# One column-block split of a product in two parts instead of three, and the order of the work around it

## The chip, the cores and the metric

One core of one Trainium2 chip. The metric is the device time of one execution in microseconds (us), median of the runs shown. Engines are named as in the profile: PE is TensorE's matrix products, PEld its weight loads, DVE VectorE, ACT ScalarE, POOL GpSimd, SP the queue that issues most DMAs.

## What is computed

Attention with a soft cap, and after it two feed-forward layers, on 896 tokens (2 sequences of 448) of width 768:

```python
scores = cap * tanh(scale * (q @ k.T) / cap);  attn = softmax(scores) @ v   # 12 heads of 64
x = attn laid out as [896, 768]
h = x @ w_in                                   # [896, 1024]
solu = h * softmax(h);  ln = layernorm(solu) * g_ln
x = ln @ w_out                                 # [896, 768]   <- the product that is changed
g = x @ w_gate;  out = (silu(g) * (x @ w_val)) @ w_out2
```

The weights come as 64-bit floats and are turned into 32-bit ones on the chip. Every large product is done as three: each operand is split into a high and a low part (`hi`, `lo`), and hi\*hi, hi\*lo and lo\*hi are added up.

## The kernel before

The program has stages that follow each other: the attention by pairs of heads, `ff1_h` (h, one of 7 token tiles of 128 at a time, on PE 36 products of 512 columns a tile), `ff1_T` (ln of a token tile is transposed into the tiles `lA`, `lB`, `lC`), `ff1_x2` (ln @ w_out), `ff2_gv` and `ff2_out`. PE leaves a result in one of 8 PSUM banks (pool `pm`); from there ACT writes the high part and DVE the low part of the transposed ln and of x.

**ln of a tile.** The tail of `ff1_h` (L354 to L391) takes the row maximum (DVE, L359), the exponentials with their sums (ACT, two halves of 512, L362), the product with h (DVE, L370), mean and variance (DVE; for tiles 5 and 6 ACT squares instead, L378), a power on POOL (L385) and the normalisation over 1024 columns (ACT for tiles 4 to 6, L388, else DVE). `ff1_T` (L395) then does 8 transposes on PE in two groups of 4, each group evicted to hi by ACT (L408) and to lo by DVE (L409). In the profile its PSUM tile is `lt`.

**w_out.** `load_w_out(j)` (L414) makes `wo_j`, the 128 output columns j of w_out, in two halves i of 512 rows each: a DMA, the conversion to 32 bits (ACT takes the absolute value, DVE clamps, shifts and joins in four instructions), four multiplications by g_ln on ACT (L422), the copy to hi on ACT (L423) and the rest to lo on DVE (L424). Rows 0 to 511 serve the contraction chunks fc 0 to 3, rows 512 to 1023 the chunks 4 to 7. Pool `wo` holds three such tiles, the raw and the 32-bit halves have two buffers each.

**The product.** `ff1_x2(j, get, N, o)` (L426) computes 128 output columns j for a block of N tokens that begins at o: 24 products (8 chunks fc times 3) of N columns, then hi by ACT (L435) and lo by DVE (L436). Before, the 896 tokens are three blocks: `lA` 384, `lB` 256, and `lC` 256, which lies in the tile `y`. That is 18 groups of 24 products.

**The order.** `steps` (L560 and L565) is the order in which the pieces are recorded. After `self.in_order = False` (L538) a scheduler moves instructions among each other, but a wait of one engine's queue holds all that stands behind it on that engine. Instructions of `load_w_out` up to the shift stay in program order (`pin=True`, L420). The stage around the change is 178.99 to 242.14 us of the trace: from the transposes of token tile 4 to the first product of `ff2_gv`.

Of the kernel before, what the change touches and what calls it, by code (L numbers as in the profile page):

```python
# [6 lines left out]
F32R = mybir.dt.float32r  # L7
# [29 lines left out]
class Kernel:  # L37
# [465 lines left out]
    def run(self):  # L503
        nc = self.nc
        KD, K1, K2, F1 = self.KD, self.K1, self.K2, self.F1
        self.raws, self.ln, self.wos, self.gvs, self.w2, self.a, self.wraw = {}, {}, {}, {}, {}, {}, {}

        st = self.st = self.pool("st", side="right")
        self.raw = self.pool("raw", side="right")
        self.at = self.pool("at", side="right")  # L510
        psc = self.psc = self.pool("psc", bufs=2, space=PSUM)
        ptA = self.pt = self.ph = self.pool("ptA", bufs=1, space=PSUM)
        self.attn_load(0, "kq")
        self.setup()
        self.w_in_load(0)
        self.attn_load(1, "kq")
        self.attn_load(0, "v")
        self.attn_load(1, "v")
        self.w_in_load(1)
        self.wi = [self.slot(f"wi{u}", [128, KD, F1], f"wi{u}") for u in range(2)]  # L520
        self.x = self.slot("x", [128, KD * 2 * 896], "x").rearrange("p (k u n) -> p k u n", k=KD, u=2)
        nc.sync.dma_start(self.gt, self.g_ln.rearrange("(f p) -> p f", p=128))


        w = [self.w_in_steps(i) for i in range(2 * KD)]
        none = lambda: None
        self.w_steps = [(w[i][1], w[i][2], w[i + 1][0] if i + 1 < 2 * KD else none, w[i][3]) for i in range(2 * KD)]
        self.attn_T(0)
        self.keep_warm(4)
        w[0][0]()  # L530
        h = [self.ff1_h(t) for t in range(7)]
        for i in range(2 * self.NP):
            self.attn_pair(i)
        self.htag = "t"
        self.attn_pair(2 * self.NP, [f for _, f in h[0][:3]])
        for _, f in h[0][3:]:
            f()
        self.in_order = False  # L538
        self.at.release()
        self.raw.release()  # L540
        ptA.release()
        psc.release()


        self.pt = self.ph = self.pool("pm", bufs=8, space=PSUM)
        self.htag, self.ttag = "m", "m"
        lA = self.slot("l", [128, K1, 2, 384], "lA")
        T = [self.ff1_T(t, lambda: lA, 128 * t) for t in range(3)]
        lp = self.pool("lp", side="right")
        self.wo = self.pool("wo", bufs=3, side="right")  # L550
        lB = lp.tile([128, K1, 2, 256], F32R, name="lB", tag="lB")
        self.y = self.slot("x", [128, KD * 2 * 896], "y")
        lC = self.y[:, :4096].rearrange("p (f u n) -> p f u n", f=K1, u=2)
        T3, T4 = self.ff1_T(3, lambda: lB, 0), self.ff1_T(4, lambda: lB, 128)
        T5, T6 = self.ff1_T(5, lambda: lC, 0), self.ff1_T(6, lambda: lC, 128)
        wo = [[(0.0, lambda j=j: self.load_w_out(j))] for j in range(KD)]
        blocks = ((lambda: lA, 384, 0), (lambda: lB, 256, 384), (lambda: lC, 256, 640))
        x2 = [[[self.ff1_x2(j, *blocks[n])] for n in range(3)] for j in range(KD)]

        steps = h[1] + T[0] + h[2] + T[1] + h[3][:2] + T[2] + h[3][2:] + h[4][:3] + wo[0] + h[4][3:] + wo[1] + h[5][:5] + T3 + h[5][5:] + h[6][:2] + T4 + h[6][2:]  # L560
        for _, f in steps:
            f()
        X = [self.slot(f"wi{u}", [128, 6144], f"x2_{u}") for u in range(2)]
        self.x2 = [X[j // 3][:, j % 3 * 1792:(j % 3 + 1) * 1792].rearrange("p (u n) -> p u n", u=2) for j in range(KD)]
        steps = x2[0][0] + x2[0][1] + wo[2] + x2[1][0] + T5 + x2[1][1] + T6 + x2[0][2] + x2[1][2]  # L565
        for j in range(2, KD):
            if j + 1 < KD:
                steps += wo[j + 1]
            if j >= KD - 2:
                steps += [(0.0, lambda i=j - KD + 2: self.load_gv(0, i))]  # L570
            steps += x2[j][0] + x2[j][1] + x2[j][2]
        for _, f in steps:
            f()
        self.wo.release()
        lp.release()


        ap = self.pool("ap", side="right")
        big = self.slot("l", [128, 6144], "a_0")
        ab = [big] + [ap.tile([128, 5376], F32R, name=f"a_{i}", tag=f"a_{i}") for i in range(1, 4)]  # L580
        w2x = self.y[:, :4608].rearrange("p (f u n) -> p f u n", f=6, u=2)
        for fc in range(K2):
            self.a[fc] = ab[fc // 3][:, fc % 3 * 1792:(fc % 3 + 1) * 1792].rearrange("p (u n) -> p u n", u=2)
        for fc in range(6):
            self.w2[0, fc] = w2x[:, fc]
        for i, t in enumerate([big] + X):
            self.w2[0, 6 + i] = t[:, 5376:].rearrange("p (u n) -> p u n", u=2)
        for fc in range(K2):
            for i, (N, o) in enumerate(((384, 0), (512, 384))):
                if fc + 1 < K2:  # L590
                    self.load_gv(fc + 1, i)
                elif i == 0:
                    for m in range(3):
                        self.w2[0, 9 + m] = self.y4(((fc - 1) % 2) * 2 + (m + 1) // 2).rearrange(
                            "p u k f -> p (u k f)").rearrange("p (m u n) -> p m u n", m=2, u=2)[:, (m + 1) % 2]
                    self.load_w2(0, 9, 1)
                    self.load_w2(0, 10, 2)
                if i == 1 and fc >= 2 and fc % 2 == 0:
                    self.load_w2(0, fc - 2, 2 if fc < 10 else 1)
                self.ff2_gv(fc, N, o)  # L600


        for fc in range(K2):
            self.w2[1, fc] = X[fc // 6][:, fc % 6 * 768:(fc % 6 + 1) * 768].rearrange("p (u n) -> p u n", u=2)
        nt = self.B * self.S // 128
        for half in range(2):
            for t in range(nt):
                if half == 0 and t < K2 // 2:
                    self.load_w2(1, 2 * t, 2)
                self.ff2_out(half, t)  # L610
        ap.release()
        st.release()
        self.pt.release()
        self.sb.release()
# [33 lines left out]
```

## Time and profile before

| | |
|---|---|
| time, median of 3 runs | 509.64 us (509.62 to 510.17) |
| the profiled execution | 509.62 us, its span 507.8 us |
| mean granted TensorE clock | 0.991 |
| PE busy | 98% of the span |
| DVE busy, ACT busy | 68%, 50% |
| DMA | 52.40 MB, mean 103 GB/s |

The span runs from the first to the last instruction of the trace; 1.8 us of the time lie around it. A busy share counts an engine as busy while any instruction of it is in work, and the end of a PE instruction is modelled, so how fast PE goes is read from the starts of its instructions. An instruction's time in the trace is longer than the distance to the next start where the two overlap; for queues that run full the distance of the starts is the cost.

### The profile page before, as it was taken

Reading aid. Unit: us, or ns where it says so; the run is one execution under the profiler, and the core shown is the slowest. Engines: PE = TensorE matmul, PEld = TensorE weight load, DVE = VectorE, ACT = ScalarE, POOL = GpSimd, SP = SyncE. Lnnn points to the kernel's source line nnn. Section 1 sums busy time; section 2 is a strip of 40 time slices with the busy share of each in tenths; the row PEclk is TensorE's granted clock in tenths of the full one; section 3 lists DMA queues with packets and bytes.
Section 4 is the critical chain, followed back from the end, with each engine's and each line's share of the span. In section 5 each row is a group of like instructions: output and inputs, shape, how many; then the busy total and the mean of one; then the engine's idle time right before and its main releaser. Section 6 shows DMA issues by size and latency. Waiting matters only on the chain.

```text
span 507.8 us, 7455 instructions
## 1 busy us (share of the span) xinstructions
PE 496.4 (98%) x2920; PEld 411.0 (81%) x2920; DVE 347.9 (68%) x625; ACT 256.4 (50%) x388; POOL 20.7 (4%) x63
## 2 busy tenths in 40 slices
PE   6999999999999999999999999999999999999996
PEld 5444544456788899999999988889999889999996
DVE  2788888873778895677899999897997868100000
ACT  2999999990313696474544444353444434100000
POOL 1111111110000000000000000000000000000000
PEclk7999999999999999999999999999999999999999
DMA  8945555310000222145354544435343525111111
GB/s 185 210 119 154 130 154 127 99 61 2 0 1 0 82 86 84 43 148 163 125 168 144 174 138 155 156 124 161 99 147 95 169 77 157 31 32 31 32 32 31
DMA packets 66916, 52.40 MB, mean 103 GB/s; under 512 B 35904, under 2 KB 62272, under 8 KB 66880
## 3 DMA queue, kind: packets, MB, share of 16 engines
q1 hardware_dynamic: 65184, 50.90, 35.6%
q10 hardware_dynamic: 1664, 1.02, 0.6%
q8 instruction: 23, 0.38, 0.3%
q14 instruction: 13, 0.11, 0.1%
q0 software_dynamic: 32, 0.00, 0.0%
HBM read 49.16 MB, written 2.75 MB: 102 GB/s over the span
## 4 chain that ended last, share of the span: by engine, by line
PE 93%; ACT 3%; DMA 2%; DVE 2%; issue 0%; ACTq 0%; POOL 0%; POOLq 0%
PE o L29 17%; PE g L29 17%; PE v L29 17%; PE x L29 10%; PE h L29 10%; PE pv L29 8%; PE sc L29 7%; PE S L29 4%; PE T L29 2%; DMA q<-in_q_dram 1%; PE lt L29 1%; ACT P L29 1%; DVE sm L29 1%; ACT wo L29 1%; DMA wo_raw<-in_moe_w_out_dram 1%; DVE e L29 0%
## 5 line engine op out<-in xcount | busy, mean ns | idle before, releaser
L29 PE MATMUL g<-x,y 128*128 128x512 f32 (+1 forms) x432 | 91.3, 363 | 0.0
L29 PE MATMUL v<-x,y 128*128 128x512 f32 (+1 forms) x432 | 90.5, 362 | 0.0
L29 PEld LDWEIGHTS g<-x,y 128*128 128x128 f32 x432 | 78.3, 188 | 8.8
L29 PEld LDWEIGHTS v<-x,y 128*128 128x128 f32 x432 | 78.2, 188 | 8.5
L29 PE MATMUL h<-wi,x 128*128 128x512 f32 x252 | 58.8, 392 | 0.0
L29 PEld LDWEIGHTS h<-wi,x 128*128 128x128 f32 x252 | 46.9, 188 | 10.9 <-issue 1.4
L29 PE MATMUL o<-x,a 128*128 128x384 f32 x294 | 52.4, 336 | 0.0
L29 PEld LDWEIGHTS o<-x,a 128*128 128x128 f32 x294 | 51.2, 188 | 0.0
L29 ACT ACTIVATE P<-sc,c 112x896 f32<-112x896 f32 x48 | 45.6, 1000 | 3.0 <-PE sc L29 2.8
L29 ACT ACTIVATE P<-P,cp 112x1792 f32<-112x1792 f32 x24 | 43.1, 1794 | 0.5
L29 PE MATMUL pv<-P,v 112*64 112x448 f32 x192 | 41.2, 551 | 0.0
L29 PEld LDWEIGHTS sc<-ks 64*112 64x112 f32 x288 | 24.0, 176 | 21.0 <-ACT P L29 9.0
L490 ACT ACTIVATE ob<-o 128x384 f32<-128x384 f32 x14 | 6.9, 494 | 65.1 <-PE o L29 65.1
L29 PE MATMUL sc<-ks 64*112 64x448 f32 x288 | 37.1, 388 | 2.0 <-ACT P L29 1.1
L29 PE MATMUL o<-y,a 128*128 128x384 f32 x189 | 34.3, 337 | 0.0
L29 PEld LDWEIGHTS o<-y,a 128*128 128x128 f32 x189 | 33.2, 188 | 0.1
L29 PEld LDWEIGHTS pv<-P,v 112*64 112x64 f32 x192 | 11.7, 136 | 23.9 <-issue 15.9
L29 PE MATMUL x<-lA,wo 128*128 128x384 f32 x144 | 28.1, 337 | 0.9 <-ACT wo L29 0.9
L29 PEld LDWEIGHTS x<-lA,wo 128*128 128x128 f32 x144 | 24.2, 188 | 1.1 <-ACT wo L29 1.1
L29 ACT ACTIVATE a<-sg 128x384 fp32r<-128x384 f32 (+1 forms) x24 | 13.8, 576 | 22.1 <-DVE sg L466 21.9
L29 ACT ACTIVATE wv<-wv_raw 128x768 f32<-128x768 f32 x12 | 10.9, 911 | 25.9 <-DMA wv_raw<-in_moe_w_val_dram 25.9
L29 DVE SCALAR_TENSOR_TENSOR w<-w_raw,w 128x768 uint32<-128x768 uint32 (+1 forms) x26 | 23.1, 892 | 0.4
(97 smaller groups left out, 681.4 us busy)
## 6 DMA issues: line engine op xcount, KB each, us to landing
wg_raw<-in_moe_w_gate_dram SPq DMA_DIRECT2D x12, 768.0 KB, 4.4
wv_raw<-in_moe_w_val_dram SPq DMA_DIRECT2D x12, 768.0 KB, 4.4
w_raw<-in_moe_w_out_dram SPq DMA_DIRECT2D x11, 768.0 KB, 4.5
wi_raw<-in_moe_w_in_dram SPq DMA_DIRECT2D x12, 512.0 KB, 4.2
wo_raw<-in_moe_w_out_dram SPq DMA_DIRECT2D x12, 512.0 KB, 3.6
k<-in_k_dram SPq DMA_DIRECT2D x24, 112.0 KB, 4.0
v<-in_v_dram SPq DMA_DIRECT2D x24, 112.0 KB, 2.8
q<-in_q_dram SPq DMA_DIRECT2D x22, 112.0 KB, 4.3
```

The costliest lines, as they stand in the source:

```text
L29: i = f(*a, **k)
L490: nc.scalar.activation(ob, acc, AF.Copy)
```

## The change

The product with w_out works on two blocks of tokens, 512 (`lA`, token tiles 0 to 3) and 384 (`lB`, tiles 4 to 6), where there were three. `lC` is gone. The order of the steps is written anew: `wo_0` and `wo_1` are recorded earlier and `wo_2` within the h stage, the transposes of tile 3 stand earlier, and the large block is done first for the column blocks 0, 1 and 2 before the small block of any of them. Then comes the small block of 0, 1 and 2, with `wo_3` to `wo_5` recorded between, then the column blocks 3 to 5 whole. The activations `a` of the second layer lie in three tiles of four where they lay in four of three; what is computed there is the same.

```diff
--- before.py
+++ after.py
@@ -544,31 +544,30 @@
 
         self.pt = self.ph = self.pool("pm", bufs=8, space=PSUM)
         self.htag, self.ttag = "m", "m"
-        lA = self.slot("l", [128, K1, 2, 384], "lA")
+        lA = self.slot("l", [128, K1, 2, 512], "lA")
         T = [self.ff1_T(t, lambda: lA, 128 * t) for t in range(3)]
         lp = self.pool("lp", side="right")
         self.wo = self.pool("wo", bufs=3, side="right")
-        lB = lp.tile([128, K1, 2, 256], F32R, name="lB", tag="lB")
+        lB = lp.tile([128, K1, 2, 384], F32R, name="lB", tag="lB")
         self.y = self.slot("x", [128, KD * 2 * 896], "y")
-        lC = self.y[:, :4096].rearrange("p (f u n) -> p f u n", f=K1, u=2)
-        T3, T4 = self.ff1_T(3, lambda: lB, 0), self.ff1_T(4, lambda: lB, 128)
-        T5, T6 = self.ff1_T(5, lambda: lC, 0), self.ff1_T(6, lambda: lC, 128)
+        T3, T4 = self.ff1_T(3, lambda: lA, 384), self.ff1_T(4, lambda: lB, 0)
+        T5, T6 = self.ff1_T(5, lambda: lB, 128), self.ff1_T(6, lambda: lB, 256)
         wo = [[(0.0, lambda j=j: self.load_w_out(j))] for j in range(KD)]
-        blocks = ((lambda: lA, 384, 0), (lambda: lB, 256, 384), (lambda: lC, 256, 640))
-        x2 = [[[self.ff1_x2(j, *blocks[n])] for n in range(3)] for j in range(KD)]
-
-        steps = h[1] + T[0] + h[2] + T[1] + h[3][:2] + T[2] + h[3][2:] + h[4][:3] + wo[0] + h[4][3:] + wo[1] + h[5][:5] + T3 + h[5][5:] + h[6][:2] + T4 + h[6][2:]
+        blocks = ((lambda: lA, 512, 0), (lambda: lB, 384, 512))
+        x2 = [[[self.ff1_x2(j, *blocks[n])] for n in range(2)] for j in range(KD)]
+
+        steps = h[1] + T[0] + h[2] + T[1] + h[3][:2] + T[2] + h[3][2:] + wo[0] + h[4][:3] + wo[1] + h[4][3:] + h[5][:2] + T3 + h[5][2:] + wo[2] + h[6][:2] + T4 + h[6][2:]
         for _, f in steps:
             f()
         X = [self.slot(f"wi{u}", [128, 6144], f"x2_{u}") for u in range(2)]
         self.x2 = [X[j // 3][:, j % 3 * 1792:(j % 3 + 1) * 1792].rearrange("p (u n) -> p u n", u=2) for j in range(KD)]
-        steps = x2[0][0] + x2[0][1] + wo[2] + x2[1][0] + T5 + x2[1][1] + T6 + x2[0][2] + x2[1][2]
-        for j in range(2, KD):
-            if j + 1 < KD:
-                steps += wo[j + 1]
-            if j >= KD - 2:
-                steps += [(0.0, lambda i=j - KD + 2: self.load_gv(0, i))]
-            steps += x2[j][0] + x2[j][1] + x2[j][2]
+        steps = x2[0][0] + x2[1][0] + T5 + x2[2][0] + T6
+        for j in range(3):
+            steps += x2[j][1] + wo[j + 3]
+        for j in range(3, KD):
+            if j > 3:
+                steps += [(0.0, lambda i=j - 4: self.load_gv(0, i))]
+            steps += x2[j][0] + x2[j][1]
         for _, f in steps:
             f()
         self.wo.release()
@@ -576,15 +575,15 @@
 
 
         ap = self.pool("ap", side="right")
-        big = self.slot("l", [128, 6144], "a_0")
-        ab = [big] + [ap.tile([128, 5376], F32R, name=f"a_{i}", tag=f"a_{i}") for i in range(1, 4)]
+        big = self.slot("l", [128, 8192], "a_0")
+        ab = [big] + [ap.tile([128, 7168], F32R, name=f"a_{i}", tag=f"a_{i}") for i in range(1, 3)]
         w2x = self.y[:, :4608].rearrange("p (f u n) -> p f u n", f=6, u=2)
         for fc in range(K2):
-            self.a[fc] = ab[fc // 3][:, fc % 3 * 1792:(fc % 3 + 1) * 1792].rearrange("p (u n) -> p u n", u=2)
+            self.a[fc] = ab[fc // 4][:, fc % 4 * 1792:(fc % 4 + 1) * 1792].rearrange("p (u n) -> p u n", u=2)
         for fc in range(6):
             self.w2[0, fc] = w2x[:, fc]
-        for i, t in enumerate([big] + X):
-            self.w2[0, 6 + i] = t[:, 5376:].rearrange("p (u n) -> p u n", u=2)
+        for i, t in enumerate([big[:, 7168:7936], X[0][:, 5376:], X[1][:, 5376:]]):
+            self.w2[0, 6 + i] = t.rearrange("p (u n) -> p u n", u=2)
         for fc in range(K2):
             for i, (N, o) in enumerate(((384, 0), (512, 384))):
                 if fc + 1 < K2:
```

Three places of the order in which the built programs issue. Names: `lt_t_g` is group g of the transposes of token tile t, `x2_j_o` the PSUM tile of column block j from token o, `wo_j` the split w_out tile, `wo_j_i` its half i in 32 bits, `wo_j_i_raw` the same as it came, `e_t` the exponentials and then ln of tile t, `h_t_f` half f of h.

**First place, PE after the last product of h.** Before, the products of the transposed tile 4 onward:

```order
L29 MATMUL lt_4_1_1798<-ident_100,e_4_1661 128x128 x4
L29 MATMUL x2_0_0_1849<-lA_1374,wo_0_1613 128x384 x14
L29 MATMUL x2_0_384_1876<-lB_1381,wo_0_1613 128x256
L29 MATMUL x2_0_0_1849<-lA_1374,wo_0_1613 128x384 x10
L29 MATMUL x2_0_384_1876<-lB_1381,wo_0_1613 128x256 x12
L29 MATMUL x2_1_0_1932<-lA_1374,wo_1_1678 128x384
L29 MATMUL x2_0_384_1876<-lB_1381,wo_0_1613 128x256 x11
L29 MATMUL x2_1_0_1932<-lA_1374,wo_1_1678 128x384 x11
L29 MATMUL lt_5_0_1959<-ident_100,e_5_1760 128x128 x4
L29 MATMUL lt_5_1_1966<-ident_100,e_5_1760 128x128 x4
L29 MATMUL x2_1_384_1973<-lB_1381,wo_1_1678 128x256 x12
```

and with the change:

```order
L29 MATMUL lt_4_1_1827<-ident_100,e_4_1690 128x128 x4
L29 MATMUL x2_0_0_1878<-lA_1374,wo_0_1593 128x512 x24
L29 MATMUL x2_1_0_1905<-lA_1374,wo_1_1642 128x512 x2
L29 MATMUL lt_5_0_1932<-ident_100,e_5_1760 128x128 x4
L29 MATMUL lt_5_1_1939<-ident_100,e_5_1760 128x128 x4
L29 MATMUL x2_1_0_1905<-lA_1374,wo_1_1642 128x512 x22
L29 MATMUL x2_2_0_1946<-lA_1374,wo_2_1777 128x512 x2
L29 MATMUL lt_6_0_1973<-ident_100,e_6_1859 128x128 x4
L29 MATMUL lt_6_1_1980<-ident_100,e_6_1859 128x128 x4
L29 MATMUL x2_2_0_1946<-lA_1374,wo_2_1777 128x512 x12
```

Behind the transposes of tile 4 there stood 48 products with `wo_0` in two blocks, one with `wo_1` among them, and the second half of `wo_1` was first used behind the transposes of tile 5; now 24 products with `wo_0` are followed by two with `wo_1`, the transposes of tile 5 and the 22 other products with `wo_1`. The first with `wo_2` come right behind.

**Second place, ACT around the eviction of tile 4's transposes.** Before:

```order
L29 ACTIVATE wo_0_1_1630<-wo_0_1_1630,gt_115 128x128 x4
L29 ACTIVATE wo_0_1613<-wo_0_1_1630 128x512
L29 ACTIVATE wo_1_0_1681<-wo_1_0_1681,gt_115 128x128 x4
L29 ACTIVATE lB_1381<-lt_4_0_1791 128x4x128
L29 ACTIVATE lB_1381<-lt_4_1_1798 128x4x128
L29 ACTIVATE wo_1_1678<-wo_1_0_1681 128x512
L29 ACTIVATE wo_1_1_1695<-wo_1_1_raw_1693 128x512
L29 ACTIVATE h_5_0_1707,sm_5_1759<-e_5_1760,sm_5_1759 128x512
L29 ACTIVATE h_5_1_1708,sm_5_1759<-e_5_1760,sm_5_1759 128x512
L29 ACTIVATE e_6_1830,sm_6_1829<-h_6_0_1777,sm_6_1829 128x512
L29 ACTIVATE e_6_1830,sm_6_1829<-h_6_1_1778,sm_6_1829 128x512
L29 ACTIVATE x2_0_1847<-x2_0_0_1849 128x384
```

and with the change:

```order
L29 ACTIVATE wo_1_0_1645<-wo_1_0_raw_1643 128x512
L29 ACTIVATE h_5_1_1708,sm_5_1759<-e_5_1760,sm_5_1759 128x512
L29 ACTIVATE lB_1381<-lt_4_0_1820 128x4x128
L29 ACTIVATE lB_1381<-lt_4_1_1827 128x4x128
L29 ACTIVATE e_6_1859,sm_6_1858<-h_6_0_1806,sm_6_1858 128x512
L29 ACTIVATE e_6_1859,sm_6_1858<-h_6_1_1807,sm_6_1858 128x512
L29 ACTIVATE e_5_1760<-e_5_1760,sm_5_1759 128x1024
L29 ACTIVATE wo_1_0_1645<-wo_1_0_1645,gt_115 128x128 x4
L29 ACTIVATE x2_0_1876<-x2_0_0_1878 128x512
L29 ACTIVATE wo_1_1642<-wo_1_0_1645 128x512
```

The scaling of the first half of `wo_1` stood ahead of the eviction of `lt_4` and its copy to hi right behind; now both stand behind the two exponentials of tile 6 and the normalisation of tile 5, and the eviction of the first x2 group stands between them.

**Third place, ACT up to the copy of the second half of `wo_1`.** Before:

```order
L29 ACTIVATE e_5_1760<-e_5_1760,sm_5_1759 128x1024
L29 ACTIVATE wo_1_1_1695<-wo_1_1_1695,gt_115 128x128 x4
L29 ACTIVATE x2_0_1847<-x2_0_384_1876 128x256
L29 ACTIVATE wo_2_0_1906<-wo_2_0_raw_1904 128x512
L29 ACTIVATE wo_1_1678<-wo_1_1_1695 128x512
```

and with the change:

```order
L29 ACTIVATE wo_1_1_1659<-wo_1_1_raw_1657 128x512
L29 ACTIVATE h_6_0_1806,sm_6_1858<-e_6_1859,sm_6_1858 128x512
L29 ACTIVATE h_6_1_1807,sm_6_1858<-e_6_1859,sm_6_1858 128x512
L29 ACTIVATE wo_2_0_1780<-wo_2_0_raw_1778 128x512
L29 ACTIVATE lB_1381<-lt_5_0_1932 128x4x128
L29 ACTIVATE lB_1381<-lt_5_1_1939 128x4x128
L29 ACTIVATE wo_1_1_1659<-wo_1_1_1659,gt_115 128x128 x4
L29 ACTIVATE e_6_1859<-e_6_1859,sm_6_1858 128x1024
L29 ACTIVATE wo_1_1642<-wo_1_1_1659 128x512
```

Between the absolute value of the second half of `wo_1` and its copy to hi now stand two squares of tile 6, the absolute value of `wo_2`'s first half, the two evictions of `lt_5`, the scaling and the normalisation of tile 6.

## Rows read from the trace of the kernel before

**Rows 1.** The page, part 1: busy time, share of the span, instructions.
```profile
PE 496.4 (98%) x2920; PEld 411.0 (81%) x2920; DVE 347.9 (68%) x625; ACT 256.4 (50%) x388; POOL 20.7 (4%) x63
```

**Rows 2.** Timeline of PE in the stage: start us, length us, instruction, count, [idle before <-releaser].
```profile
178.99 1.03 PE L29 MATMUL lt<-ident,e 128*128 128x128 f32 x8
179.78 2.67 PE L29 MATMUL x<-lA,wo 128*128 128x384 f32 x14
...
188.97 1.03 PE L29 MATMUL lt<-ident,e 128*128 128x128 f32 x8
...
194.80 1.03 PE L29 MATMUL lt<-ident,e 128*128 128x128 f32 x8
196.20 0.50 PE L29 MATMUL x<-y,wo 128*128 128x256 f32 x2 [0.37 <-ACT y L29]
...
215.29 1.31 PE L29 MATMUL x<-y,wo 128*128 128x256 f32 x10
217.54 0.62 PE L29 MATMUL x<-lA,wo 128*128 128x384 f32 x2 [0.94 <-ACT wo L29]
...
232.34 2.25 PE L29 MATMUL x<-lA,wo 128*128 128x384 f32 x12
...
242.14 3.29 PE L29 MATMUL g<-x,y 128*128 128x384 f32 x18
```

**Rows 3.** Timeline of PE in the gate and value products.
```profile
259.80 3.28 PE L29 MATMUL v<-x,y 128*128 128x384 f32 x18
262.92 4.28 PE L29 MATMUL g<-x,y 128*128 128x512 f32 x18
267.04 4.24 PE L29 MATMUL v<-x,y 128*128 128x512 f32 x18
```

**Rows 4.** Timeline of ACT around the end of the h stage.
```profile
178.34 1.26 ACT L29 ACTIVATE wo<-wo,gt 128x128 f32<-128x128 f32 x4
179.62 1.09 ACT L29 ACTIVATE lB<-lt 128x512 fp32r<-128x512 f32 x2
180.59 0.63 ACT L29 ACTIVATE wo<-wo 128x512 fp32r<-128x512 f32 x1
181.11 0.67 ACT L29 ACTIVATE wo<-wo_raw 128x512 f32<-128x512 f32 x1
181.67 0.70 ACT L29 ACTIVATE h<-e,sm 128x512 f32<-128x512 f32 x1
...
183.08 0.69 ACT L29 ACTIVATE e<-h,sm 128x512 f32<-128x512 f32 x1
...
184.41 0.50 ACT L29 ACTIVATE x<-x 128x384 fp32r<-128x384 f32 x1
184.78 1.26 ACT L29 ACTIVATE e<-e,sm 128x1024 f32<-128x1024 f32 x1
185.91 1.28 ACT L29 ACTIVATE wo<-wo,gt 128x128 f32<-128x128 f32 x4
```

**Rows 5.** Timeline of DVE, ln of tile 3 and the end of h.
```profile
160.87 0.81 DVE L29 TENSOR_SCALAR e<-e,sm 128x1024 f32<-128x1024 f32 x1
...
179.09 0.69 DVE L29 TENSOR_REDUCE sm<-h 128x1 f32<-128x512 f32 x1
179.69 0.68 DVE L29 TENSOR_TENSOR wo<-wo,wo 128x512 fp32r<-128x512 f32 x1
...
182.93 0.42 DVE L29 TENSOR_SCALAR wo<-wo 128x512 f32<-128x512 f32 x1
...
183.84 0.69 DVE L29 SCALAR_TENSOR_TENSOR wo<-wo_raw,wo 128x512 uint32<-128x512 uint32 x1
```

**Rows 6.** Stretches: us, busy (instructions) by engine, PEclk, DMA share, GB/s.
```profile
6.00:8.00 2.00, 0.74 (x5) 0.59 (x6) 0.00 (x0) 0.00 (x0) 0.00 (x0) 0.85 1.19 254
8.00:14.00 6.00, 5.18 (x27) 3.54 (x27) 3.82 (x7) 2.51 (x4) 0.00 (x0) 0.50 1.28 219
...
178.99:242.14 63.15, 61.84 (x457) 61.37 (x456) 45.89 (x95) 42.07 (x99) 1.47 (x2) 1.00 0.33 104
```

## The prediction

> **What bounds the kernel now.** The page's busy shares come first: PE works in 98% of the span, DVE in 68%, ACT in 50% [rows 1]. So time is saved only where PE waits or where its products get shorter, and any new wait of PE is paid in full. The change sits in one stage, 178.99 to 242.14 us, 63.15 us in all. The timeline of PE shows what that stage is made of [rows 2]. Eight transposes take 0.79 us from start to start (178.99 to 179.78). One column block, 72 products in three token blocks, takes 9.80 us (232.34 to 242.14), and six of them 58.8 us. PE was late twice: behind the transposes of tile 6 it started 1.40 us after their start instead of 0.79 (0.6 us, for the copy into y), and the ten 256-column products at 215.29 were followed by a start 2.25 us later where ten of them need some 1.2 (1.0 us, for a copy of w_out by ACT). Transposes 2.4, products 58.8 and waits 1.6 make 62.8 of the 63.15 us; the small rest stays open. The granted clock was 1.00 throughout the stage, the 2.4 GHz level [rows 6].
>
> The timeline of ACT is the view that decides here [rows 4]. In the stage ACT is busy 42.07 of 63.15 us [rows 6], but around the end of h its queue is full: each instruction starts before the last one's end. There the distances of the starts are the price of an instruction: four scalings by g_ln 1.2 to 1.3 us, two evictions of a transposed tile 0.97, a copy to hi 0.52, an absolute value of 512 columns 0.56, two squares 1.41 (181.67 to 183.08), two exponentials 1.33 (183.08 to 184.41), a normalisation 1.13 (184.78 to 185.91).
>
> **Part 1, the shorter products.** Per column block and chunk there were three groups of 384, 256 and 256 columns; there are two of 512 and 384. The gate and value products show the new sizes at work: 18 products of 384 columns take 3.12 us, or 173 ns each, 18 of 512 take 4.12 us, or 229 ns [rows 3]. 6 column blocks of 24 products of each size: 144 x (0.229 + 0.173) = 57.9 us against 58.8. That is 0.9 us less, from 432 products that become 288. The Trainium skill (TensorE: Matmul & The Clock Gate, "Wait — 56ns, not 53.3ns?") gives a warm product a fixed cost of about 2.5 ns besides its columns. By that rule 144 products fewer save an estimated 0.4 us, and my sum would end half a microsecond later. The rows of this kernel, at the sizes in question, say 0.9, and I take them.
>
> **Part 2, the order.** Tile 3's transposes move ahead of ten products of h, some 2.3 us. Before, ln of tile 3 was ready at 161.7 us [rows 5], seventeen us before the stage, so that is free: the h products stay back to back and the stage begins at the same time. The old two waits fall away: y is no longer a target, and blocks 3 to 5 of w_out are now made while PE does 72 products of the small block, 12.5 us, where ACT needs about 4.6 us for one (twice 0.56 + 1.2 + 0.52).
>
> What is late next is `wo_1`, then `wo_2`. I count from the first transpose of tile 4 (t = 0) and go along the queues in the order that the changed program shows.
>
> PE: transposes 0.79, 24 products with `wo_0` 5.50. At t = 6.3 it asks for the high part of `wo_1`'s first half.
>
> DVE, from t = 0.1: row maximum, rest of `wo_0`, row maximum, a clamp, a tiny step, the rest of tile 4, the last maximum of tile 6: four times 0.60 (179.09 to 179.69), 0.4 and some 0.3 for the tiny ones [rows 5]. So tile 6's exponentials can start on ACT at t = 3.2. ACT is in order: exponentials 1.33, normalisation of tile 5 1.13, scaling 1.2, the eviction of the first x2 group 0.5 (the trace has no eviction of 512 columns of x; 0.37 for 384 and 0.49 for a 512-column group of transposes bound it), the copy 0.63 to its end. That is t = 8.0. **First wait: 1.7 us.**
>
> PE then does two products (0.46), tile 5's transposes (0.8) and ten products (2.3), and at t = 11.6 asks for the second half of `wo_1`. ACT, from the start of the copy at t = 7.4: copy 0.52, absolute value 0.56, two squares 1.41, absolute value of `wo_2` 0.56, two evictions 0.97, scaling 1.2, normalisation of tile 6 1.13, copy 0.63. That is t = 14.4. **Second wait: 2.8 us.** The third product needs the low part, which DVE writes 0.68 us behind the copy, while PE has two products of 0.46 in hand: with the hand-over another **0.4 us**.
>
> Then `wo_2`: PE does 10 + 2 products, the transposes of tile 6 and 10 more, and reaches its second half at t = 21.1. On ACT and DVE that half is a chain of its own: copy 0.52, a wait for DVE's joining of the first half 0.4, scaling 1.3, copy 0.54, absolute value 0.7, on DVE two steps of 0.42 and two of 0.69 with the gaps that dependent steps show [rows 5], 2.4, then scaling 1.2, an eviction 0.5, copy 0.63. It ends at t = 22.0. **Third wait: 0.9 us.**
>
> The sum: transposes 2.4, products 57.9, waits 1.7 + 2.8 + 0.4 + 0.9 = 5.8 us make a stage of 66.1 us against 63.15, or **2.9 to 3.0 us more**. Behind the stage everything hangs on PE's full rows, so it is passed on whole. The second layer's other tile shapes hold the same data and I cost them at nothing; what covers them is that g is not evicted until 18 + 18 products later. The profiled execution took 509.62 us and is the median of 509.64 within 0.02, so I predict 512.6 us.
>
> Bounds: the last copy of `wo_2` ends some 22 us after t = 0. All ends hang on sums of queue distances, and 5% of 22 us is 1.1 us either way: 511.5 to 513.7. A gain in these sums is possible, since the scalings lie between 1.2 and 1.3; a loss, since hand-overs between engines are counted at some 0.05 us.
>
> **Rivals.** *The clock falls (16%).* In the first microseconds PE was busy only 0.74 of 2 us, the clock fell, and it stayed at 0.50, the 1.2 GHz level, for at least 6 us although PE was busy 5.18 of those [rows 6]. Waits of 1.7 and 2.8 us so close together leave PE idle for a large part of some 8 us. If the clock falls as at the start, up to half of 6 us is lost. The third wait hides 0.9 of that, since `wo_2` does not hang on PE. That gives 512.6 + 2.1 = 514.7; if it is back after half as long, 513.2. Against it: at 1.00 PE stood 1.0 us idle without a fall [rows 2], and between the waits it runs dense products. The Trainium skill (TensorE: Matmul & The Clock Gate, "Why this matters for your kernels") warns of idle gaps between bursts of products that bring the half clock back; no trace here shows a gap of this length in dense work.
>
> *The other side: faster, `wo_1` and `wo_2` in time (6%).* If the two halves land before PE asks, nothing of the 5.8 us is left: 2.4 + 57.9 + 0 against 63.15, so 506.8. The point from which it decides: the copy of `wo_1`'s second half must be ready at t = 11.6, not 14.4. For it: ACT stands idle about 1.5 us before tile 6's exponentials, and only 42 of 63 us are busy. Against it: that idle time cannot be used, as ACT takes its queue in order and the exponentials stand ahead. The Trainium skill (Perfetto Trace Analysis, "Matmuls") prefers larger products to smaller ones; by that alone the result would be this one.
>
> *The waits are half as long (6%).* If the chains run some 2.5 us ahead of my sums, through a DVE that reaches the maxima earlier, about 2.5 to 3 us of waits are left and the time is 509.3 to 509.8, no difference. It needs more than 10% on each row I used.
>
> **How the numbers follow.** Forecast 72%, clock 16%, faster 6%, half 6%. The likeliest gives 512.6. The range of 511.2 to 514.8 takes in the bounds of the sums and the clock's full price; the two cases below it are left out. A measurement of this kernel can tell about 0.2%, 1 us, from no change: slower 0.88, same 0.06, faster 0.06.
>
> **What would show it.** In the changed profile: products of x in two forms, 144 of 512 and 144 of 384 columns, starts 227 to 229 and 173 ns apart; PE idle before x for some 5 to 6 us in all, ended by ACT's `wo` (three times) and DVE's `wo`; the stage about 66 us long; no idle time for y, nor a wait for blocks 3 to 5; PEclk 9 in every slice but the first. It is wrong if PE idles under 3 us there, if the stage begins later than 179 us, or if PEclk drops within it.

## The result and the profile after

The changed kernel takes 513.12 us (median, 513.08 to 513.28) where the kernel before takes 509.9 on the same chip: a ratio of 1.0062 (95% interval 1.0051 to 1.0074), some 3.2 us slower. 512.6 was forecast, in a range of 511.2 to 514.8. The profiled execution took 513.08 us with a span of 511.3, against 509.62 and 507.8, so 3.5 us are to be found.

Part 1 of the page of the changed kernel, in the order of [rows 1]:

```profile
PE 497.3 (97%) x2776; PEld 404.8 (79%) x2776; DVE 347.7 (68%) x619; ACT 255.3 (50%) x382; POOL 20.9 (4%) x63
```

PE's busy time is as before, within 0.9 us, though 144 of its instructions are gone; the span is 3.5 us longer. The time is in what PE waits for. The timeline of PE in the same stage, columns as in [rows 2]:

```profile
179.07 1.04 PE L29 MATMUL lt<-ident,e 128*128 128x128 f32 x8
179.86 5.76 PE L29 MATMUL x<-lA,wo 128*128 128x512 f32 x24
186.93 0.73 PE L29 MATMUL x<-lA,wo 128*128 128x512 f32 x2 [1.32 <-ACT wo L29]
187.50 1.04 PE L29 MATMUL lt<-ident,e 128*128 128x128 f32 x8
188.29 2.54 PE L29 MATMUL x<-lA,wo 128*128 128x512 f32 x10
193.25 3.83 PE L29 MATMUL x<-lA,wo 128*128 128x512 f32 x14 [2.42 <-ACT wo L29]
196.92 1.03 PE L29 MATMUL lt<-ident,e 128*128 128x128 f32 x8
197.71 2.54 PE L29 MATMUL x<-lA,wo 128*128 128x512 f32 x10
200.70 0.73 PE L29 MATMUL x<-lA,wo 128*128 128x512 f32 x2 [0.45 <-ACT wo L29]
...
235.49 2.92 PE L29 MATMUL x<-lA,wo 128*128 128x512 f32 x12
...
245.20 2.96 PE L29 MATMUL g<-x,y 128*128 128x384 f32 x16
```

Two waits stand there by name, 1.32 and 2.42 us, and a third of 0.45. As starts they are larger, since a product's modelled end hides part of a wait: 24 products of 0.229 us behind 179.86 would end at 185.36, and PE started at 186.93 (1.57 us); ten behind 188.29 at 190.58, and PE started at 193.25 (2.67); the 14 behind it took 3.67 us instead of 3.21 (0.46); ten behind 197.71 would end at 200.00, and PE started at 200.70 (0.70). Together 5.4 us. The old waits of [rows 2], behind tile 6 and at 217.54, are gone. The waits of PE and its weight loads in this stretch, by who ended them (total us, times, longest):

```profile
PEld x L29 <- ACT wo L29: 5.5, 3, 2.8
PE x L29 <- ACT wo L29: 4.2, 3, 2.4
...
PEld x L29 <- DVE wo L29: 0.5, 1, 0.5
```

ACT's copies of w_out ended three of them and DVE's low part the fourth, as each step had it. ACT's timeline over the first two, against [rows 4]:

```profile
182.14 0.69 ACT L29 ACTIVATE e<-h,sm 128x512 f32<-128x512 f32 x1 [1.35 <-DVE sm L29]
...
183.48 1.24 ACT L29 ACTIVATE e<-e,sm 128x1024 f32<-128x1024 f32 x1
184.61 1.27 ACT L29 ACTIVATE wo<-wo,gt 128x128 f32<-128x128 f32 x4
...
186.26 0.62 ACT L29 ACTIVATE wo<-wo 128x512 fp32r<-128x512 f32 x1
...
189.32 1.06 ACT L29 ACTIVATE lB<-lt 128x512 fp32r<-128x512 f32 x2
190.28 1.27 ACT L29 ACTIVATE wo<-wo,gt 128x128 f32<-128x128 f32 x4
191.44 1.23 ACT L29 ACTIVATE e<-e,sm 128x1024 f32<-128x1024 f32 x1
192.57 0.62 ACT L29 ACTIVATE wo<-wo 128x512 fp32r<-128x512 f32 x1
```

The lines left out are full as well: this queue has no gap worth the name from 182.14 to the copy at 192.57 that PE waits for. The scaling of `wo_1`'s first half (184.61) stands behind tile 6's exponentials and tile 5's normalisation, the copy (186.26) ends at 186.88, and PE starts at 186.93. The second copy ends at 193.19, and PE starts at 193.25.

The stage as a stretch (columns as in [rows 6]):

```profile
178.99:245.50 66.51, 62.26 (x316) 54.54 (x314) 47.51 (x91) 40.37 (x92) 1.42 (x2) 1.00 0.31 99
```

The granted clock stayed at 1.00: waits of 1.6 and 2.7 us did not bring it down. From the first transpose of tile 4 to the first product of g the stage lasts 245.20 - 179.07 = 66.13 us where it lasted 63.15: 3.0 of the 3.5 us. Another 0.4 us lies at the very end, in products that the prediction costed at nothing more than before. The chain of waits of the kernel before has one row for all products of o (start, length, count):

```profile
415.96 87.87 PE o L29 x504
```

and that of the changed kernel:

```profile
419.00 88.29 PE o L29 x504
```

The 504 products have the same shapes and take 0.42 us longer.

### The profile page after: what moved, and what is told of

Same layout as the page of the kernel before. It is cut to its first block, busy times and chain, and to the rows that moved or that the text cites. A ratio compares the mean times of both kernels' runs of the same rounds, so it can differ in the third digit from the quotient of the medians.

```text
span 511.3 us, 7160 instructions
## 1 busy us (share of the span) xinstructions
PE 497.3 (97%) x2776; PEld 404.8 (79%) x2776; DVE 347.7 (68%) x619; ACT 255.3 (50%) x382; POOL 20.9 (4%) x63
## 4 chain that ended last, share of the span: by engine, by line
PE 91%; DVE 4%; ACT 2%; DMA 1%; issue 0%; ACTq 0%; POOL 0%; DVEq 0%; POOLq 0%
PE o L29 17%; PE g L29 17%; PE v L29 17%; PE h L29 10%; PE x L29 9%; PE pv L29 8%; PE sc L29 7%; PE S L29 4%; PE T L29 2%; DVE wo L29 2%; DMA q<-in_q_dram 1%; DVE sm L29 1%; ACT wo L29 1%; ACT e L29 1%; PE lt L29 1%; DVE ks L29 1%
## 5 line engine op out<-in xcount | busy, mean ns | idle before, releaser
L29 PE MATMUL h<-wi,x 128*128 128x512 f32 x252 | 58.8, 392 | 0.0
L29 PE MATMUL x<-lA,wo 128*128 128x512 f32 x144 | 36.9, 397 | 4.2 <-ACT wo L29 4.2
L29 PEld LDWEIGHTS x<-lA,wo 128*128 128x128 f32 x144 | 26.4, 188 | 10.4 <-ACT wo L29 5.5
L29 PE MATMUL x<-lB,wo 128*128 128x384 f32 x144 | 27.2, 335 | 0.0
L29 PEld LDWEIGHTS x<-lB,wo 128*128 128x128 f32 x144 | 25.3, 188 | 1.2 <-ACT lB L29 0.2
```

The costliest lines, as they stand in the source:

```text
L29: i = f(*a, **k)
```

## The experiments

Theory W: the loss is PE's wait for the halves of `wo_1` and `wo_2`, which ACT's and DVE's queues finish too late for a block that asks for them after 24 products. Rivals: P, the products or the layout cost more; O, the new order of the h stage by itself holds things up; C, w_out earlier means ln later.

A table of the stages of each profiled execution, from the starts of PE (h is its first product of tile 0, T4 the first transpose of tile 4; us):

| kernel | h to T4 | T4 to g | g to o | products of o | time, median | ratio to before (95%) |
|---|---|---|---|---|---|---|
| before | 66.62 | 63.15 | 173.65 | 87.68 | 509.64 | |
| the change | 66.66 | 66.13 | 173.64 | 88.10 | 513.12 | 1.0062 (1.0051 to 1.0074) |
| w_out recorded earlier | 66.63 | 61.06 | 173.64 | 88.11 | 507.85 | 0.9958 (0.9946 to 0.9971) |
| without the scaling | 66.71 | 60.95 | 173.60 | 88.10 | 508.43 | 0.9970 (0.9961 to 0.9980) |
| order alone | 66.65 | 63.03 | 173.65 | 87.68 | 509.80 | 1.0001 (0.9992 to 1.0010) |
| layout of a alone | 66.67 | 63.05 | 173.65 | 88.10 | 509.98 | 1.0005 (0.9996 to 1.0014) |
| two blocks alone | 66.66 | 64.98 | 173.64 | 88.11 | 512.34 | 1.0055 (1.0042 to 1.0068) |
| recorded too early | 72.74 | 63.11 | 173.64 | 88.11 | 515.22 | 1.0104 (1.0082 to 1.0125) |
| earlier, squares on ACT | 66.66 | 61.08 | 173.64 | 88.10 | 508.20 | 0.9971 (0.9962 to 0.9979) |
| the same, padded | 66.67 | 61.66 | 173.64 | 88.11 | 508.07 | 0.9966 (0.9954 to 0.9978) |
| three blocks, earlier | 66.64 | 62.24 | 173.65 | 87.68 | 508.95 | 0.9981 (0.9972 to 0.9989) |

What is not in these columns, the start of the program, differs by up to a microsecond between executions; the columns repeat within some 0.1 us wherever nothing was changed in them, T4 to g excepted, where the last wait for w_out varies (shown with the padding below). So differences of stages are read from the trace, and the times are read with their intervals. A ratio compares all runs of a kernel with all runs of the kernel before on the same chip (medians of 509.70 to 509.90 us), so it is not the quotient of two times of the column.

**w_out recorded earlier.** Blocks and products of the change, one line of order moved:

```diff
-steps = ... + T[1] + h[3][:2] + T[2] + h[3][2:] + wo[0] + h[4][:3] + wo[1] + h[4][3:] + ... + h[5][2:] + wo[2] + h[6][:2] + ...
+steps = h[1] + T[0] + h[2] + wo[0] + T[1] + h[3][:2] + T[2] + wo[1] + h[3][2:] + h[4] + wo[2] + h[5][:2] + T3 + h[5][2:] + h[6][:2] + T4 + h[6][2:]
```

> The changed kernel with one line different: wo_0 is recorded behind the h products of tile 2, wo_1 behind the transposes of tile 2 and wo_2 behind the h products of tile 4, each some 8 to 12 us earlier than in the change. Blocks, products and layouts stay. Theory W (the loss is PE's wait for the halves of wo_1 and wo_2, which ACT and DVE finish too late): the lost starts of 1.6, 2.7, 0.5 and 0.7 us before products of x go, 5.4 us in all, and the time is 513.1 - 5.4 = 507.7 us, under both kernels. Theory P (the 512-column products, their tiles or the layout cost more than the rows of before said): the waits may go, but the time stays at 512 to 513. Rival C (the early conversion of w_out holds up ln of the token tiles on DVE): a new wait before a transpose takes the place of the old ones, 509 to 513.

Measured: 507.85 us, ratio 0.9958: faster than both kernels, and within 0.2 us of W's 507.7. The timeline of PE in its stage:

```profile
178.31 1.03 PE L29 MATMUL lt<-ident,e 128*128 128x128 f32 x8
179.10 11.25 PE L29 MATMUL x<-lA,wo 128*128 128x512 f32 x48
190.19 1.03 PE L29 MATMUL lt<-ident,e 128*128 128x128 f32 x8
190.98 3.00 PE L29 MATMUL x<-lA,wo 128*128 128x512 f32 x12
...
198.24 12.13 PE L29 MATMUL x<-lB,wo 128*128 128x384 f32 x69
```

48 products of 512 columns run without a gap where the change had three waits among them: 190.19 - 179.10 = 11.09 us, or 231 ns each. In the change 24 products took the 7.07 us from 179.86 to 186.93, and ten took the 4.96 us from 188.29 to 193.25; both stretches are gone. The stage is 66.13 - 61.06 = 5.07 us shorter, and ln of the tiles is not late either (h to T4 66.63). W holds, and C falls; P falls for this stage, whose products and tiles are those of the change (for the products of o it does not, see the layout of a).

**Without the scaling.** The four multiplications on ACT are taken out of `load_w_out`:

```diff
-            for m in range(4):
-                self.A.activation(f[:, m], f[:, m], AF.Copy, scale=self.gt[:, 4 * i + m:4 * i + m + 1])
```

> The changed kernel without the four multiplications of each half of w_out by g_ln on ACT (so the output lacks g_ln): 1.2 us of ACT less for each half, nothing else taken away; the order is the scheduler's own again. Theory W: with 1.2 us less in front of the copies and a shorter queue between them the waits before x go almost wholly, stage some 5 us shorter, 507.6 us; a wait of 0.3 us for wo_2 may be left. Theory P: PE's products are as long as before, and the time stays within 1 us of 513.1. If the halves were late through their DMA and not through ACT, the time stays as well and the waits are ended by the DMA's wo_raw.

Measured: 508.43 us, stage 60.95, 5.2 us shorter than the change's. PE's timeline:

```profile
180.10 8.50 PE L29 MATMUL x<-lA,wo 128*128 128x512 f32 x36
188.44 1.03 PE L29 MATMUL lt<-ident,e 128*128 128x128 f32 x8
189.23 5.77 PE L29 MATMUL x<-lA,wo 128*128 128x512 f32 x24
```

The waits are gone by taking 1.2 us of ACT from each half; the scheduler also puts ten more products ahead of tile 5's transposes. That ACT's queue was late, and not the DMA, is seen from the loads of `wo_1`, which landed at 168.87 and 177.74 in the change and at 169.01 and 177.41 here: in the change ACT took the second half at 186.78, nine us after it had landed. The loads of `wo_2` do start some 3 us earlier here, so for them this run alone does not part the two; in the change its second half landed at 193.51, and ACT took it at 195.26, straight behind a copy.

**The order alone.** The kernel before, its three blocks kept, with the order of the change in the h stage:

```diff
-steps = ... + h[3][2:] + h[4][:3] + wo[0] + h[4][3:] + wo[1] + h[5][:5] + T3 + h[5][5:] + h[6][:2] + T4 + h[6][2:]
+steps = ... + h[3][2:] + wo[0] + h[4][:3] + wo[1] + h[4][3:] + h[5][:2] + T3 + h[5][2:] + wo[2] + h[6][:2] + T4 + h[6][2:]
...
-steps = x2[0][0] + x2[0][1] + wo[2] + x2[1][0] + T5 + ...
+steps = x2[0][0] + x2[0][1] + x2[1][0] + T5 + ...
```

> The kernel before, its three token blocks kept, with the change's order of the h stage alone: wo_0 and wo_1 recorded earlier, wo_2 within the h stage, tile 3 transposed earlier. Theory W: three blocks give PE 48 products with wo_0 before it needs wo_1 for good, so the same late halves are met later: some 2.0 us of waits in place of 1.6, 509.6 to 510.0 us, no difference to before. Rival O (the new order by itself holds up the h stage or the evictions): 511 to 513 us with the old blocks too. Theory P also says no difference to before.

Measured: 509.80 us, ratio 1.0001. O falls: with 48 products behind the first half the late halves are met in time, as was forecast. One wait moved to another place; PE's timeline:

```profile
190.01 1.35 PE L29 MATMUL x<-lB,wo 128*128 128x256 f32 x10
192.77 1.09 PE L29 MATMUL lt<-ident,e 128*128 128x128 f32 x8 [1.42 <-ACT e L29]
```

It is ln of tile 6 that is late for its transposes by 1.42 us: ACT normalises it behind its squares, work on `wo_2` and `wo_1` and the evictions of tile 5; the old waits are gone, and the sum stays.

**Two blocks alone.** The changed kernel with w_out and tile 3's transposes recorded where they were before:

```diff
-steps = ... + h[3][2:] + wo[0] + h[4][:3] + wo[1] + h[4][3:] + h[5][:2] + T3 + h[5][2:] + wo[2] + h[6][:2] + T4 + h[6][2:]
+steps = ... + h[3][2:] + h[4][:3] + wo[0] + h[4][3:] + wo[1] + h[5][:5] + T3 + h[5][5:] + h[6][:2] + T4 + h[6][2:]
...
-steps = x2[0][0] + x2[1][0] + T5 + x2[2][0] + T6
+steps = x2[0][0] + wo[2] + x2[1][0] + T5 + x2[2][0] + T6
```

> The changed kernel with the order of the kernel before in the h stage: the two token blocks alone. wo_0, wo_1 and tile 3's transposes stand where they stood, wo_2 behind the first group of x. Theory W, with waits summed along the queues of this order: 1.7 us for the first half of wo_1, 1.1 for its low part, 0.9 and 0.3 for wo_2, 4.0 us in place of the change's 5.4 to 5.8, so 511.1 to 511.7 us: slower than before, less slow than the change. The block split is then what asks too early, and the new order of the h stage adds to it. Rival O (the order recorded for the h stage is the whole loss): 507.5 to 508.5 us.

Measured: 512.34 us, above the range that was given, ratio 1.0055. The direction holds (slower than before, less than the change), the size does not quite. PE's timeline:

```profile
188.53 1.03 PE L29 MATMUL lt<-ident,e 128*128 128x128 f32 x8
190.97 0.74 PE L29 MATMUL x<-lA,wo 128*128 128x512 f32 x2 [1.41 <-ACT wo L29]
192.61 5.32 PE L29 MATMUL x<-lA,wo 128*128 128x512 f32 x22 [0.90 <-DVE wo L29]
197.76 1.03 PE L29 MATMUL lt<-ident,e 128*128 128x128 f32 x8
199.17 3.29 PE L29 MATMUL x<-lA,wo 128*128 128x512 f32 x12 [0.37 <-ACT wo L29]
```

Behind tile 5's transposes PE starts 2.44 us after them instead of 0.79 (1.65 us), the next wait is 1.18, behind tile 6 it is 0.62; with the small ones 4.3 us where 4.0 were summed, 1.1 less than the change's 5.4. The stage is 1.15 us shorter than the change's; the times alone do not part the two, as the intervals of their ratios overlap. So the split by itself makes most of the waits, and the new order of the h stage, which costs nothing with three blocks, adds the smaller share with two.

**Three blocks, earlier.** The question left: is the split worth anything once no half is late?

```diff
-steps = x2[0][0] + x2[0][1] + wo[2] + x2[1][0] + T5 + x2[1][1] + T6 + x2[0][2] + x2[1][2]
+steps = x2[0][0] + x2[0][1] + x2[1][0] + T5 + x2[1][1] + T6 + x2[0][2] + wo[3] + x2[1][2] + wo[4]
...
-            if j + 1 < KD:
-                steps += wo[j + 1]
+            if j + 3 < KD:
+                steps += wo[j + 3]
```

with the first list of the h stage as in the kernel with w_out earlier.

> The kernel before with its three token blocks, but with the earlier records of w_out (wo_0 behind h of tile 2, wo_1 behind the transposes of tile 2, wo_2 behind h of tile 4) and each later block of w_out recorded as soon as its buffer comes free. This shows what the split in two blocks is worth once no half of w_out is late. Theory W with the rows' products: 58.8 us of products and one wait of 0.6 to 0.9 us for y behind the transposes of tile 6, against 58.3 and no wait with two blocks; so 508.6 to 509.0 us, some 1 us under the kernel before and 0.8 to 1.2 above the two blocks with the same earlier records (507.85). If the split is worth nothing, 507.9; if the gain of the earlier records comes only together with two blocks, 509.8.

Measured: 508.95 us, ratio 0.9981, as forecast, and a stage of 62.24 us. PE behind the transposes of tile 6:

```profile
195.13 1.03 PE L29 MATMUL lt<-ident,e 128*128 128x128 f32 x8
196.67 0.50 PE L29 MATMUL x<-y,wo 128*128 128x256 f32 x2 [0.50 <-ACT y L29]
```

Two blocks with the same early w_out have 61.06: the split is worth 1.2 us of the stage, of which 0.75 us is the wait for y (1.54 us from tile 6's transposes to the next product, for 0.79) that is left with three blocks in this order. The layout of a that comes with the two blocks gives 0.4 back in the products of o.

**Recorded too early.** The changed kernel with w_out a step earlier still, behind the transposes of tiles 0 and 1 and h of tile 3:

```diff
-steps = h[1] + T[0] + h[2] + T[1] + h[3][:2] + T[2] + h[3][2:] + wo[0] + h[4][:3] + wo[1] + h[4][3:] + ... + h[5][2:] + wo[2] + h[6][:2] + ...
+steps = h[1] + T[0] + wo[0] + h[2] + T[1] + wo[1] + h[3][:2] + T[2] + h[3][2:] + wo[2] + h[4] + ... + h[5][2:] + h[6][:2] + ...
```

> The changed kernel with wo_0 recorded behind the transposes of tile 0, wo_1 behind those of tile 1 and wo_2 behind the h products of tile 3, one token tile earlier still than in the kernel that was 5 us faster. Theory W with its condition: the waits for wo_1 and wo_2 are gone here too, but DVE's conversion of wo_0 stands in front of ln of tile 1, and PE waits 3.3 us for it before the transposes of tile 1; later 0.8 us for lB and 1.7 us for wo_3: 512.9 us. Rival (the earlier the better, since ACT is idle for most of the h stage): 507 to 508 us. The clock: a wait of 3.3 us in dense work is longer than any so far; if it fell, the stretch behind it would show 0.50 and the time would be some 2 us longer.

Measured: 515.22 us (512.95 to 516.65), the slowest of all; the rival's 507 to 508 us falls, and W's 512.9 was 2.3 us too low, about what a fall of the clock costs. DVE first, around tile 1:

```profile
137.35 0.88 DVE L29 TENSOR_SCALAR wo<-wo 128x512 f32<-128x512 f32 x2
...
142.39 0.68 DVE L29 TENSOR_TENSOR wo<-wo,wo 128x512 fp32r<-128x512 f32 x1
...
146.19 0.81 DVE L29 TENSOR_SCALAR e<-e,sm 128x1024 f32<-128x1024 f32 x1
```

Clamps and low part of `wo_0` (137.35, 142.39) run between the steps of tile 1's ln, which is normalised only at 146.19. PE's timeline:

```profile
135.55 8.45 PE L29 MATMUL h<-wi,x 128*128 128x512 f32 x36
147.06 1.97 PE L29 MATMUL lt<-ident,e 128*128 128x128 f32 x8 [3.06 <-DVE e L29]
148.68 10.46 PE L29 MATMUL h<-wi,x 128*128 128x512 f32 x36
158.97 1.03 PE L29 MATMUL lt<-ident,e 128*128 128x128 f32 x8
```

PE waits for it, and then the 36 products of h behind take 10.29 us (148.68 to 158.97) where 36 x 0.229 us make 8.2. The stretches say why (PEclk in the column behind the engines):

```profile
142.00:146.20 4.20, 2.00 (x9) 1.31 (x7) 3.92 (x12) 0.50 (x1) 0.56 (x1) 1.00 0.21 71
146.20:153.00 6.80, 5.94 (x18) 5.08 (x19) 6.54 (x14) 4.67 (x12) 0.00 (x0) 0.50 0.23 77
153.00:160.00 7.00, 7.00 (x36) 5.86 (x35) 4.39 (x11) 2.87 (x7) 0.99 (x1) 1.00 0.24 77
```

The clock fell to 0.50, the 1.2 GHz level, for the stretch from 146.2 to 153: PE had been busy 2.00 of the 4.20 us before, and stood still when it fell, 2.2 us into the wait of 3.06 that began at 144.00. From tile 1's transposes to tile 2's it took 158.97 - 147.06 = 11.91 us, where transposes of 0.79 and 36 products of 8.24 make 9.03: the fall cost 2.9 us. The profiled execution took 516.21 us, so an estimated 513.3 without the fall. The six runs spread over 3.7 us. One of them, at 514.23 us, had a mean granted clock of 0.999, which leaves no room for 6.8 us at half, so between executions the fall costs some 2 us, give or take the microsecond by which starts differ; of the others the mean clock does not say where it was low. So the rival of the falling clock is real in this program, at a wait of 3.06 us and not at the change's of 1.32 and 2.42. The length of a wait alone does not decide it here, as the fall came 2.2 us into this one and the change's 2.42 us passed without.

**Squares on ACT.** The kernel with w_out earlier, and in it the squares of tile 4 on ACT too, not on DVE:

```diff
-            sq = t >= 5
+            sq = t >= 4
```

> The kernel with the earlier records of w_out (wo_0 behind h of tile 2, wo_1 behind the transposes of tile 2, wo_2 behind h of tile 4) and the squares of tile 4 on ACT too, as those of tiles 5 and 6 are (t >= 4 for t >= 5): 1.2 us of bn_stats less on DVE. Theory W: the small waits that were left there (0.2 us beyond the transposes' own 0.8 before x behind tile 6) go, and the first to wait is ln of tile 0 alone: 507.0 to 507.8 us. Rival C (ACT, now with two squares more, is late with a copy): 508 to 509 us.

Measured: 508.20 us, stage 61.08. No gain over 61.06: neither W's small gain nor C's loss shows in the stage, though 508.20 lies in C's range, and the times (ratios 0.9958 and 0.9971) overlap at their ends. Theory W expected small waits to go; one of 0.2 us for the last column block of w_out came in their place (starts at 235.09 and 235.64, where two products of 0.173 us lie between).

**The layout of a.** The kernel before with a in three tiles of four chunks, as the change has it, and lA, which shares the first one's place, in a slot of that size:

```diff
-        lA = self.slot("l", [128, K1, 2, 384], "lA")
+        lA = self.slot("l", [128, 8192], "lA")[:, :6144].rearrange("p (f u n) -> p f u n", f=K1, u=2)
...
-        big = self.slot("l", [128, 6144], "a_0")
-        ab = [big] + [ap.tile([128, 5376], F32R, name=f"a_{i}", tag=f"a_{i}") for i in range(1, 4)]
+        big = self.slot("l", [128, 8192], "a_0")
+        ab = [big] + [ap.tile([128, 7168], F32R, name=f"a_{i}", tag=f"a_{i}") for i in range(1, 3)]
...
-            self.a[fc] = ab[fc // 3][:, fc % 3 * 1792:(fc % 3 + 1) * 1792].rearrange("p (u n) -> p u n", u=2)
+            self.a[fc] = ab[fc // 4][:, fc % 4 * 1792:(fc % 4 + 1) * 1792].rearrange("p (u n) -> p u n", u=2)
...
```

> The kernel before with the change's layout of the second layer's activations alone: three tiles of four chunks for a where there were four of three, and the tile that lA lies in as large as in the change. The trace of the change shows the last 252 products of o 0.45 us longer in sum than before (175.2 ns from start to start where there were 173.4). If that comes from where a lies, the time is 510.1 us and these starts are 175 to 176 ns apart. If it is a difference between executions of one kernel, the time is 509.7 and the starts stay at 173.4 or differ from run to run. Theory W makes no statement on it; the waits before x stay as in the kernel before.

Measured: 509.98 us, ratio 1.0005, which does not tell it from no change; the trace does. The chain's row for o:

```profile
415.79 88.29 PE o L29 x504
```

against the kernel with the order alone, whose a lies as before:

```profile
415.64 87.86 PE o L29 x504
```

In the chains of all eleven kernels of the table, a in three tiles goes with 88.29 us and in four with 87.86 or 87.87, whatever the stages before did. So 0.42 us of the change's loss come with this layout. The timeline of PE says in which products, the second 252 of the 504; first the kernel with the layout, then the one with the order alone:

```profile
459.59 44.48 PE L29 MATMUL o<-x,a 128*128 128x384 f32 x252
459.46 44.03 PE L29 MATMUL o<-x,a 128*128 128x384 f32 x252
```

From start to start these are 175.9 ns apart where they were 174.1 (251 distances in 44.14 and 43.69 us), which is the slower pace that was forecast. The first 252, which have the same `a` as their stationary operand and other tiles of w_out2 as the moving one, are 174.5 ns apart with either layout. So where `a` lies does not by itself explain it. The edit also enlarges the slot that `lA` and `a` share and moves a piece of w_out2, and these were not tested apart.

**Padding.** The kernel with squares on ACT, and its second and third tile of a larger by 1024 bytes, which moves what lies behind them by 1024 and 2048:

```diff
-        ab = [big] + [ap.tile([128, 7168], F32R, name=f"a_{i}", tag=f"a_{i}") for i in range(1, 3)]
+        ab = [big] + [ap.tile([128, 7424], F32R, name=f"a_{i}", tag=f"a_{i}") for i in range(1, 3)]
```

> The same kernel with 256 columns of padding behind each of the two later tiles of a, which moves their addresses by 1024 and 2048 bytes and nothing else. The last 252 products of o took 44.14 us in every kernel whose a lies in three tiles and 43.69 us where it lies in four, whatever stood before them. If the address within 2048 bytes decides, the products of chunks 8 to 11 (the tile moved by 1024) fall from 175.8 to 173.3 ns and the time by 0.2 us; if the distance or the tile's size decides, they stay at 175.8 ns and the time is that of the kernel without padding.

Measured: 508.07 us, and the row of the chain:

```profile
413.98 88.29 PE o L29 x504
```

Nothing changed in o, so shifts of the two later tiles by 1024 and 2048 bytes do not decide. What does was not found. Its stage T4 to g is 0.6 us longer than that of the kernel without padding, by one wait for the last column block of w_out. PE's timeline:

```profile
234.94 0.51 PE L29 MATMUL x<-lB,wo 128*128 128x384 f32 x2
236.03 2.57 PE L29 MATMUL x<-lA,wo 128*128 128x512 f32 x10 [0.58 <-DVE wo L29]
```

In this kernel's chain that low part stands on DVE behind work on the gate weights, and that behind their transfer, which landed at 229.93. The kernel without padding has the same order and 0.2 us of this wait. So the sixth block's readiness varies by some tenths, and differences of this size between the faster kernels are not to be read as effects of their edits.

## Why the prediction was right

**What bounds it.** Right: PE, and every new wait of it was paid. From the first product of g to the first of o it takes 173.65 us before and 173.64 after, so the delay is passed on whole.

**Part 1, shorter products.** The sum had 57.9 us; 66.13 less 5.4 of waits and 2.4 of transposes leaves 58.4. The last column block takes 9.71 us (235.49 to 245.20) for 48 products where 24 x (0.229 + 0.173) make 9.65, and the others are alike. The gain over 58.8 is 0.4 to 0.5 us, not 0.9 (six times 9.80 - 9.71 make 0.5). The rule of the Trainium skill that I set aside (TensorE: Matmul & The Clock Gate, "Wait — 56ns, not 53.3ns?") gives an estimate of 0.4. The total comes near it, though not by the rule's own terms: the 512-column products are 227 to 231 ns apart, 14 to 18 more than 512 columns at 2.4 GHz take.

**Part 2, the order.** The stage begins when it did (66.66 against 66.62 from h), tile 3's move was free, the two old waits are gone, and blocks 3 to 5 of w_out are in time. The chain came out in sequence and in size. From the first transpose (179.07): exponentials forecast at 3.2, measured 3.07; PE at its first half forecast 8.0, measured 7.86; at the second 14.4 and 14.18; at `wo_2` 22.0 and 21.63. The waits: 1.7, 2.8, 0.4, 0.9 forecast, 1.57, 2.67, 0.46, 0.70 measured. That is 0.4 us less than forecast and cancels the 0.4 of part 1, so the stage came out at 66.1 as summed. The chain was understood; that the sum met to a tenth is luck. The rest of 0.35 us that the prediction left open before is not in its sum, and hardly anything of it is left after.

**What was missed.** "The second layer's other tile shapes hold the same data and I cost them at nothing": this step failed, by 0.42 us. The reason given with it spoke of the eviction of g and not of the products of o; they take longer with the new layout, and why stays open. Without it the time would have been an estimated 512.7 us, for 512.6 forecast.

**The rivals.** The clock did not fall here; the kernel recorded too early shows the same mechanism at a longer wait, with a price of 2.9 us within its execution, where the prediction had up to 3.0. The faster side needed `wo_1` ready at t = 11.6, and the kernels that have it so take 507.85 and 508.43 us where the rival had 506.8; most of the difference is the 0.4 to 0.5 us by which part 1 gained less, and the 0.42 us of o.

## What to carry to other kernels

Fewer and larger products ask for their next operand sooner: before a block is made larger, sum along the queue of the engine that prepares that operand what stands in front of it, from starts and not from durations, and compare with the moment at which the matrix engine arrives. Preparing it earlier pays only as long as the preparing engines have room; w_out recorded about a token tile earlier gained 5 us, a step more lost 7. An engine that is 40% idle over a stage can still be late at every point of it that counts.

## What the runs showed of the hardware

The products of o, same count and shape, take 87.87 us with `a` in four tiles and 88.29 with it in three, in all eleven kernels. The difference lies in the last 252, 174.1 against 175.9 ns from start to start; the first 252 keep their pace of 174.5. Moving two of the tiles by 1024 and 2048 bytes did not change it, and the cause is not known.

The clock fell to half 2.2 us into a wait of 3.06 us in otherwise dense work, and stayed there for 6.8 us although PE was busy 5.94 of them; waits of 1.32 and 2.42 us, with twelve products and a set of transposes between them, left it at 1.00.
